# Halving the matmuls of an inverse row product by exchanging partitions with DMA

## The chip, the cores and the metric

One core of one Trainium2 chip. The metric is device time in microseconds (us) of one execution. A run gets a state: "slow" when it is over 1.5% above the fastest run of the same kernel, else "fast"; causes are read from fast runs. In the lines of the profile `ps` is a PSUM buffer, in which TensorE leaves its results, and `arena` the kernel's SBUF buffer, spread over 128 partitions; an *eviction* copies from `ps` to `arena`. SPq and ACTq are the issuing of transfers by SyncE and ScalarE. Where I name a ratio, it is the mean time of one kernel's fast runs over the mean of the other's fast runs of the same rounds, so it is not quite the ratio of the medians that stand beside it.

## The reference, cut to what matters

```python
xn = layernorm(A_x)                                   # 2048 x 640
X  = rfft2(xn)                                        # 2048 x 321, complex
y  = irfft2(X * (w_r + 1j * w_i), s=(2048, 640))      # the spectral filter
h  = (xn @ w_gate) * (xn @ w_up)                      # 640 -> 1536
out = A_x + y + h @ w_down                            # 2048 x 640
```

The kernel writes the transforms as matmuls with constant tables. The rows are split 2048 = 64 x 32. In the *spectrum stage* 16 steps each handle two groups of frequencies ("g" 0 and 1): a column product (forward), a forward row product, the filter product with the weights, and an inverse row product. Gate/up products are mixed in to fill TensorE.

## The kernel before: what the change touches

For every group the kernel multiplied the row product's PSUM result with both weights, real and imaginary, and formed the inverse as two accumulating passes over them. GpSimd, with some help of ScalarE and VectorE, made the negated copies that this needs.

```python
def em_wm(...):                       # VectorE, from PSUM, for one group q
    for h in range(2):                # 4 of 5 column classes, both weights at once
        c.e.tensor_tensor(dst, xh.unsqueeze(1).to_broadcast([128, 2, 32, 4]), wv, _OP.mult)
    return c.e.tensor_tensor(d5, x5, wg[:, :, 0:321:5], _OP.mult)      # the fifth class
def em_ng(...):                       # GpSimd, ScalarE or VectorE: negated copy
def em_ns(...):                       # GpSimd: two copies and a negation of 63 to 65 columns
def em_ia(...):                       # TensorE: ten matmuls for one group
    for k in range(5):
        l1, l2 = (yg[:, 578 + k:1090:4], yg[:, 322 + k:834:4]) if k < 4 else (yg[:, 0:128], yg[:, 128:256])
        c.e.matmul(dst, l1, v_ti[:, q, 0, :], start=True, stop=False)
        ins = c.e.matmul(dst, l2, v_ti[:, q, 1, :], start=False, stop=True)
# (cut: weights loaded straight from w_r and w_i, two to four transfers for each and every two steps)
# The order on each engine comes from a list planner in the kernel, which counts
_DMA_ISSUE = 500.0    # ns for SyncE to issue a transfer
_DMA_LAT = 1150.0     # ns from the last byte to the waiting engine
```

## Time and profile before

| | before |
|---|---|
| time, median of 3 (range) | 204.56 us (204.50 to 204.68) |
| TensorE busy | 198.0 us, 98% |
| VectorE / ScalarE / GpSimd busy | 89% / 63% / 16% |
| spectrum stage, 82.6 to 138.5 us | 55.9 us, TensorE busy 55.2 |

The lines and their reading are in the prediction.

### The profile page before, as it was taken

The numbers are of one execution on the slowest core, as the hardware profiler recorded it, in microseconds if no ns is written. First come the engines' busy times: TensorE is split into PE (matmuls) and PEld (weight loads), VectorE is DVE, ScalarE is ACT, GpSimd is POOL, SyncE is SP. The second block draws the span as 40 slices with busy tenths as digits, with TensorE's granted clock in tenths as the row PEclk, the third lists the DMA queues.
The fourth block names the chain that finished last, engine by engine and source line by source line (L and its number), as shares of the span: only waits on it lengthen the run. The fifth ranks groups of instructions, "written<-read, shape, count | busy, mean of one in ns | idle before, by whom it ended". The sixth has DMA issues, their size and how long they took to land.

```text
span 202.8 us, 4769 instructions
## 1 busy us (share of the span) xinstructions
PE 198.0 (98%) x1785; PEld 128.1 (63%) x1785; DVE 179.5 (89%) x511; ACT 127.5 (63%) x277; POOL 32.0 (16%) x108
## 2 busy tenths in 40 slices
PE   7999999999999999899999999999999999999995
PEld 7987644454444555556666666667777767777774
DVE  3599999999999997697988898864999999999983
ACT  3678899999975776869999999987611220200000
POOL 0000000000000000075754675453000000000000
DMA  6999983031161597605354444004313332332222
GB/s 183 300 341 378 377 80 65 3 65 32 32 63 39 112 276 194 197 14 132 74 145 114 103 102 127 0 5 136 92 32 97 106 107 66 113 90 81 93 65 65
DMA packets 31542, 23.82 MB, mean 117 GB/s; under 512 B 10528, under 2 KB 29472, under 8 KB 31392
## 3 DMA queue, kind: packets, MB, share of 16 engines
q1 hardware_dynamic: 30720, 23.16, 43.5%
q10 hardware_dynamic: 800, 0.36, 0.6%
q8 instruction: 14, 0.23, 0.5%
q14 instruction: 8, 0.07, 0.1%
HBM read 18.92 MB, written 2.62 MB: 106 GB/s over the span
## 4 chain that ended last, share of the span: by engine, by line
PE 85%; DVE 5%; SPq 4%; DMA 4%; issue 1%; ACT 1%
PE ps L978 44%; PE ps L1237 23%; SPq L712 4%; DMA arena<-in_A_x_dram 4%; PE ps L1131 3%; PE ps L1130 3%; PE ps L998 2%; PE ps L1079 2%; PE ps L938 2%; PE ps L1159 2%; PE ps L1249 2%; PE ps L1056 2%; DVE arena L719 1%; DVE arena L1257 1%; DVE arena L1186 0%
## 5 line engine op out<-in xcount | busy, mean ns | idle before, releaser
L718 ACT ACTIVATE arena<-ps 128x512 bf16<-128x512 f32 (+7 forms) x206 | 104.8, 547 | 40.1 <-PE ps L1159 24.0
L978 PE MATMUL ps<-arena 128*128 128x512 bf16 x420 | 97.0, 379 | 0.1
L978 PEld LDWEIGHTS ps<-arena 128*128 128x128 bf16 x420 | 38.9, 98 | 41.9 <-ACT arena L718 1.4
L1237 PE MATMUL ps<-arena 128*128 128x320 bf16 (+2 forms) x396 | 56.5, 295 | 0.2 <-DVE arena L1257 0.2
L1237 PEld LDWEIGHTS ps<-arena 128*128 128x128 bf16 x396 | 37.6, 98 | 13.9 <-DVE arena L1257 0.5
L1094 DVE TENSOR_TENSOR arena<-ps,arena 128x256 bf16<-128x256 f32 x64 | 24.0, 416 | 0.1
L1014 DVE TENSOR_TENSOR arena<-arena 128x512 bf16<-128x512 bf16 x42 | 17.7, 421 | 4.7 <-ACT arena L718 4.7
L1107 POOL TENSOR_SCALAR arena<-arena 128x256 bf16<-128x256 bf16 x8 | 6.8, 855 | 89.3 <-DVE arena L1097 89.2
L719 DVE CAST arena<-ps 64x321 bf16<-64x321 f32 (+1 forms) x25 | 12.2, 490 | 6.3 <-PE ps L1131 5.8
L1257 DVE TENSOR_TENSOR arena<-ps,arena 128x320 bf16<-128x320 f32 (+2 forms) x33 | 15.4, 473 | 1.8 <-PE ps L1249 1.8
L998 PE MATMUL ps<-arena 128*128 128x128 bf16 (+1 forms) x160 | 14.4, 246 | 0.4 <-ACT arena L718 0.4
L1130 PEld LDWEIGHTS ps<-arena 128*128 128x128 bf16 x160 | 12.4, 114 | 2.8 <-ACT arena L718 0.4
L998 PEld LDWEIGHTS ps<-arena 128*128 128x128 bf16 x160 | 12.0, 98 | 2.1 <-ACT arena L718 1.2
L1130 PE MATMUL ps<-arena 128*128 128x64 bf16 x160 | 13.3, 196 | 0.0
L1131 PE MATMUL ps<-arena 128*128 128x64 bf16 x160 | 13.3, 197 | 0.0
L1131 PEld LDWEIGHTS ps<-arena 128*128 128x128 bf16 x160 | 11.2, 113 | 2.1
L1116 POOL TENSOR_SCALAR arena<-arena 128x65 bf16<-128x65 bf16 x32 | 12.1, 378 | 0.0
L1114 POOL COPY arena<-arena 128x63 bf16<-128x63 bf16 x32 | 8.6, 268 | 17.1 <-DVE arena L1097 17.0
L1097 DVE TENSOR_TENSOR arena<-ps,arena 128x130 bf16<-128x130 f32 x32 | 9.3, 292 | 0.0
L776 ACT ACTIVATE arena<-arena 128x640 bf16<-128x640 bf16 x11 | 9.1, 824 | 0.0
L1115 POOL COPY arena<-arena 128x63 bf16<-128x63 bf16 x32 | 9.0, 280 | 0.0
L891 DVE TENSOR_TENSOR arena<-arena 128x384 f32<-128x384 bf16 x16 | 8.8, 552 | 0.0
(62 smaller groups left out, 221.0 us busy)
## 6 DMA issues: line engine op xcount, KB each, us to landing
arena<-in_A_x_dram SPq DMA_DIRECT2D x20, 160.0 KB, 2.4
out_dram<-arena SPq DMA_DIRECT2D x31, 80.0 KB, 1.6
arena<-in_A_w_r_dram SPq DMA_DIRECT2D x8, 160.5 KB, 3.0
arena<-in_A_w_i_dram SPq DMA_DIRECT2D x8, 160.5 KB, 3.0
arena<-in_B_w_gate_dram SPq DMA_DIRECT2D x4, 320.0 KB, 5.8
arena<-in_A_x_dram SPq DMA_DIRECT2D x1, 1280.0 KB, 9.8
arena<-in_A_w_r_dram SPq DMA_DIRECT2D x14, 80.2 KB, 2.9
arena<-in_A_w_i_dram SPq DMA_DIRECT2D x14, 80.2 KB, 3.1
```

Source lines behind the costliest of these rows:

```text
L718: return c.e.activation(dst, src, _ACTF.Copy)
L719: return c.e.tensor_copy(dst, src)
L978: ins = c.e.matmul(ps[:, bk, :], v_gw[:, w, j, ft, :], v_xt[:, j, rows], start=(j == 0), stop=(j == 4))
L998: ins = c.e.matmul(ps[:, bk, w * n:(w + 1) * n], v_gw[:, w, j, ft, :], v_xt[:, j, rows], start=(j == 0), stop=(j == 4))
L1014: return c.e.tensor_tensor(v_ht[:, ft0, rows], v_gbf[:, rr, 0, :], v_gbf[:, rr, 1, :], _OP.mult)
L1094: c.e.tensor_tensor(dst, xh.unsqueeze(1).to_broadcast([128, 2, 32, 4]), wv, _OP.mult)
L1097: return c.e.tensor_tensor(d5, x5, wg[:, :, 0:321:5], _OP.mult)
L1116: return c.e.tensor_scalar(yg[:, 128:193], yg[:, 256:321], -1.0, None, _OP.mult)
L1130: c.e.matmul(dst, l1, v_ti[:, q, 0, :], start=True, stop=False)
L1131: ins = c.e.matmul(dst, l2, v_ti[:, q, 1, :], start=False, stop=True)
L1237: ins = c.e.matmul(ps[:, bk, 0:sl3.stop - sl3.start], v_ht[:, ft, a * 128:(a + 1) * 128], v_wd[:, ft, sl3], start=(ft == _FT_ORDER[0]), st ...
L1257: return c.e.tensor_tensor(v_out[:, a % 2, sl3], ps[:, bk, 0:sl3.stop - sl3.start], v_xr[:, xs, sl3], _OP.add)
```

## The change

The intent: do the inverse in one pass, 160 matmuls in place of 320. One pass needs both parts of the product, which lie in different partitions, so the parts are brought together by DMA: the imaginary product is sent to its neighbour partition and added, and the mirrored half is fetched from the other 64 partitions. For this the weights have to lie in filter order with a sign for each partition; a one-time rearrangement through DRAM (26 copies) gives the order, and GpSimd multiplies the sign in. The last additions also move from VectorE to ScalarE copies with a bf16 addition. The diff, cut to its core:

```diff
-for g in range(2): em_wm, em_ng (negate), em_ns (copies), em_ia with ten matmuls
+d_w2 = nc.dram_tensor("w_slots", [2, _R // 2, 64, 2, 321], _BF).ap()
+for i_, (dst_, src_) in enumerate(prep):                      # 26 copies DRAM to DRAM, forward stage
+    dma("wprep%d" % i_, dst_, src_, ...)
+def em_ws(c, wi=v_wr[wr][:, :, 1, :]):                        # GpSimd, 8 times, 128 x 1284
+    return c.e.tensor_scalar(wi, wi, v_tau, None, _OP.mult)
+                                                              # VectorE: 4 products of 320, 2 of 4 (em_wa, em_wb)
+for i_ in range(2):                                           # first exchange: neighbours
+    dma("sw%d_%d" % (t, i_), qs[i_:128:2, :, 0:322], yb[1 - i_:128:2, :, 322:644], ...)
+def em_sum(c, yb=yb, qs=qs):                                  # VectorE
+    return c.e.tensor_tensor(yb[:, :, 0:322], yb[:, :, 0:322], qs[:, :, 0:322], _OP.add)
+for i_, (pd, psr, gs, k_) in enumerate(mv):                   # second exchange: halves (2 issues, 7 in step 0)
+    dma("ng%d_%d" % (t, i_), yb[pd, gs, 321:640], yb[psr, gs, 1:320], ...)
+def em_ia(...):                                               # TensorE: ten matmuls for BOTH groups
+            ins = c.e.matmul(ps[...], yb[:, g, o_:o_ + 636:5], v_ti[:, 2 * t + g, :], start=True, stop=True)
(cut: tables, buffers, order of the down weights, final additions)
```

## The prediction

> **What bounds the kernel now.** I read the page's busy shares first, then the chain that ended last, then the table of busy time by stage, then the timeline inside the stage that is rewritten.
>
> ```profile
> PE 198.0 (98%) x1785; PEld 128.1 (63%) x1785; DVE 179.5 (89%) x511; ACT 127.5 (63%) x277; POOL 32.0 (16%) x108
> ...
> PE 85%; DVE 5%; SPq 4%; DMA 4%; issue 1%; ACT 1%
> PE ps L978 44%; PE ps L1237 23%; SPq L712 4%; DMA arena<-in_A_x_dram 4%; PE ps L1131 3%; PE ps L1130 3%; PE ps L998 2%; PE ps L1079 2%; PE ps L938 2%; PE ps L1159 2%; PE ps L1249 2%; PE ps L1056 2%; DVE arena L719 1%; DVE arena L1257 1%; DVE arena L1186 0%
> ```
>
> TensorE is busy for 98% and carries 85% of the chain; no other engine has more than 5%. L978 is the gate/up product, L1237 the down product, and L1130/L1131 the two passes of the inverse row product, which the change halves.
>
> The stage table (us; PE, PEld, DVE, ACT, POOL busy, then clock, DMA share, GB/s):
>
> ```profile
> 18.00:82.60 64.60, 64.32 (x381) 32.89 (x382) 61.55 (x185) 54.43 (x116) 0.00 (x0) 1.00 0.54 128
> 82.60:138.50 55.90, 55.22 (x670) 34.16 (x667) 47.40 (x146) 51.33 (x119) 31.71 (x104) 1.00 0.35 88
> 138.50:163.40 24.90, 24.82 (x227) 18.66 (x224) 22.53 (x54) 8.28 (x14) 0.12 (x1) 1.00 0.30 87
> 163.40:202.80 39.40, 36.90 (x295) 27.02 (x293) 35.61 (x86) 2.60 (x4) 0.00 (x0) 1.00 0.28 84
> ```
>
> I call them forward, spectrum, combine and end. TensorE idles 0.3, 0.7, 0.1 and 2.5 us in them (the 2.5 is the last addition and store). So a change gains only by taking TensorE work away, and it loses whatever idle time it opens. The spectrum stage has VectorE (47.4) and ScalarE (51.3) close behind.
>
> The price of one inverse-row matmul is its spacing, not its duration:
>
> ```profile
> 104.98 0.19 PE L1130 MATMUL ps<-arena 128*128 128x64 bf16 x1
> 105.01 0.20 PE L1131 MATMUL ps<-arena 128*128 128x64 bf16 x1
> 105.04 0.20 PE L1130 MATMUL ps<-arena 128*128 128x64 bf16 x1
> ...
> 105.27 0.19 PE L1131 MATMUL ps<-arena 128*128 128x64 bf16 x1
> ```
>
> The ten start 32 ns apart. The groups view says 196 ns each, because these matmuls overlap.
>
> **What the Trainium skill says.** "TensorE: Matmul & The Clock Gate", "Wait — 56ns, not 53.3ns?", puts the warm spacing at N/2.4 ns plus 2.5 ns. For N=64 that is 29 ns; the trace has 32 ns here and 31 ns for the five of L1056. So the count of matmuls sets the price.
>
> "VectorE: DVE Perf Modes", "The perf-mode tier table", has any product with a float32 PSUM operand at one element a cycle and a bf16 tensor-tensor in SBUF at two. The trace agrees:
>
> ```profile
> L1094 DVE TENSOR_TENSOR arena<-ps,arena 128x256 bf16<-128x256 f32 x64 | 24.0, 416 | 0.1
> L1014 DVE TENSOR_TENSOR arena<-arena 128x512 bf16<-128x512 bf16 x42 | 17.7, 421 | 4.7 <-ACT arena L718 4.7
> L1097 DVE TENSOR_TENSOR arena<-ps,arena 128x130 bf16<-128x130 f32 x32 | 9.3, 292 | 0.0
> ```
>
> "SBUF — State Buffer", "SBUF: two separate sides", says GpSimd and a VectorE instruction with two SBUF inputs take a shared port pair in turn, for a whole instruction. The trace shows one direction: a GpSimd copy beside the VectorE product of L1014 is stretched from 0.23 to 0.44 us, while L1014 keeps its 0.42.
>
> ```profile
> 106.30 0.43 DVE L1014 TENSOR_TENSOR arena<-arena 128x512 bf16<-128x512 bf16 x1
> 106.38 0.44 POOL L1115 COPY arena<-arena 128x63 bf16<-128x63 bf16 x1
> ```
>
> The other direction, VectorE held by a long GpSimd instruction, is not in this trace, because GpSimd's are short.
>
> "DMA: Bandwidth & Descriptors", "Why a DMA increments its semaphore by 16 and not by 1", says a copy runs on the largest number of engines up to 16 that divides both outer dimensions. That explains the blocks of 15 or 16 outer rows. No run yet shows it.
>
> **The change, part by part.**
>
> *Inverse row product.* 320 matmuls become 160: 160 x 32 ns = 5.1 us off TensorE, all in the spectrum stage and on the chain (L1130 and L1131 hold 3% + 3% there, about 10.5 us for all 320). The forward matmuls widen from 321 to 326 columns: 32 x 5/2.4 ns = 0.07 us more. Everything else on TensorE keeps its count. Stage floor 55.9 - 5.1 = 50.8 us, or 3.2 us for each of the 16 steps.
>
> *VectorE in the spectrum stage.* From the timeline, spacing is the duration less about 80 ns: 0.34 us for L1094, 0.20 for L1097, 0.34 for L1014. Before: 64 x 0.34 + 32 x 0.20 for products, 18 x 0.34 for the gate products, 8 x 0.18 negations, 18 x 0.41 and 7 x 0.42 evictions: 46 us. After, one step has four products of 320 from PSUM (320/0.96 ns + 70 = 0.40 us), two of four elements (about 0.1) and one bf16 sum of 644 (644/2/0.96 ns + 70 = 0.40): 2.2 us, 16 times, 35.4. With 18 gate products (6.1) and the 14 evictions that the new order leaves it (5.7): 47 us. So VectorE goes from 46 of 55.9 to 47 of 50.8, 93%.
>
> *ScalarE.* It loses 16 negations (6.7 us). It takes all inverse evictions, 16 of 640 at about 0.70 us (11.2) in place of 25 of 320 at 0.436 (10.9), and 50 forward evictions in place of 46 (+1.7): 51.3 becomes about 47 of 50.8.
>
> *GpSimd.* 104 short instructions go. Eight sign products over 128x1284 come: 256 elements took 855 ns and 65 took 378, so 2.5 ns an element and 216 ns fixed: 3.4 us each, 27 us.
>
> *Exchanges.* A step now crosses partitions twice by DMA: product, exchange, sum, exchange, inverse. An 80 KB store here lands 1.6 us after issue and a 160 KB load in 2.4:
>
> ```profile
> arena<-in_A_x_dram SPq DMA_DIRECT2D x20, 160.0 KB, 2.4
> out_dram<-arena SPq DMA_DIRECT2D x31, 80.0 KB, 1.6
> ```
>
> Each exchange is two issues of 80 KB, so about 2.4 us from first issue to last landing. Chain of one step: 0.3 forward + 1.4 three products + 2.4 + 1 queueing + 0.4 sum + 2.4 + 0.5 = 8.4 us. The new order puts an inverse just ahead of the fourth forward product after its own, 3 to 4 steps or 9.5 to 12.7 us later. It fits, with 1 to 4 us spare.
>
> *Rearrangement.* 5.3 MB go through DRAM once more, during the forward stage, where DMA carries 20 to 70 GB/s. Bytes are no problem; order is. The first two copies are issued ahead of the last transpose that the second group of rows needs:
>
> ```profile
> 31.08 2.52 SPq L837 DMA_TRANSPOSE arena<-arena  x2
> ```
>
> That transpose leaves at 32.4 and lands by about 35.5; its matmuls begin near 37.2 (60 matmuls of 0.216 us and three short groups from 23.1). Two copies cost about 2 us to issue and 2 to 4 to move. The transpose then lands at 37 to 40: 0 to 3 us of idle TensorE, middle 1.
>
> *End.* Final additions: 30 products from PSUM (0.48 us) leave VectorE for 30 ScalarE copies and 15 bf16 additions (about 0.49): VectorE gains 7 us. TensorE is already busy there except for the tail, so 0 us. The down product may start before the inverse is done, behind which the last step's exchanges hide: four gate/up groups (4.3 us) and 20 down matmuls (2.7) stand between.
>
> *Sum.* 204.56 - 5.1 + 0.1 = 199.5 with no new idle time. I add 1 us for the transpose and 1 us for exchanges caught behind a weight load: each load is 330 KB into 64 partitions, two every other step, queued ahead of exchanges that have 1 to 4 us spare. Prediction 201.6.
>
> **The rivals.**
>
> *Everything hides: 199.5.* For it: 1 to 4 us spare in the chain, ScalarE relieved, seven eighths of the order unchanged. Against: it needs no idle time in a stage with VectorE at 93%.
>
> *The exchange latency becomes the bound.* Transfers run in one order on one issuing queue; one that waits for VectorE holds those behind it. If the chain takes 14 us and four spectrum buffers are in use, a step takes 3.5 us in place of 3.2: 16 x 0.3 = 5 us, time 204 to 206. For it: four buffers and two issues for every hop. Against: the hops measure 1.6 to 2.4 us.
>
> *GpSimd holds VectorE.* If a 3.4 us sign product blocks the next two-input VectorE instruction until it ends, each of about five in the stage costs some 2.3 us, 11 us on an engine with 3.5 spare: 8 us more, 208 to 210. For it: the skill's lock. Against: in the trace GpSimd is the one that waits, and VectorE keeps its 0.42 us.
>
> **Range and chances.** The floor of 199.5 can hardly be beaten, since TensorE's other work is the same; 198.6 allows for its present 1.1 us of idle before the tail. The top, 207, holds the latency rival and half of the GpSimd one. To be faster by over 2% (below 200.5) needs less than 1 us of new idle time: 0.33. Slower by over 2% (above 208.7) needs the GpSimd lock or a serial chain: 0.11. Between: 0.56.
>
> **What would show it.** Right: 160 inverse matmuls 32 ns apart; TensorE's sum about 193 us; spectrum stage 51 to 53 us from the first forward product to the last inverse; PSUM products of 320 near 0.48 us and the bf16 sum near 0.49; exchanges landing in under 2.5 us; sign products near 3.4 us, with L1014's successor still near 0.42. Wrong: TensorE waiting in the spectrum stage on a partition exchange for several us (latency), gate products or sums stretched to 1 us or more beside a sign product (lock), or matmuls near 37 us waiting on the transpose for more than 3 us. A time below 198.6 would mean that TensorE had hidden idle time that I counted as work.

## The result, and the profile after

The changed kernel is correct and took 230.89 us (median of 4, 227.33 to 233.07) against 204.53 (204.25 to 204.68) in the same rounds: ratio 1.117, 95% interval 1.110 to 1.123. I had predicted 201.6 and a range up to 207. Two of the four runs are slow; the two fast ones (227.33 and 229.76, middle 228.55) are 24 us slower than before.

The profiled execution of the changed kernel fell in the slow state (231.3 us span); profiles of its variants that did not (no_prep, sign_tiny and sign_vector below) show the same picture in the parts that they keep, so I read it for where the time lies and take sizes from the fast runs. Its page has, in the same places as before, the busy shares and the chain by engine:

```profile
PE 205.2 (89%) x1625; PEld 126.3 (55%) x1625; DVE 184.0 (80%) x492; ACT 139.5 (60%) x287; POOL 28.7 (12%) x12
...
DVE 32%; PE 30%; DMA 18%; SPq 12%; ACT 3%; issue 3%; POOL 2%; DVEq 0%; POOLq 0%
```

The number of matmuls fell by 160 as meant. But TensorE went from 85% of the chain to 30%; DMA and SyncE's issuing (SPq) together have 30%, and VectorE 32%. No engine is full on average. This is the mark of a chain of waits that goes from engine to engine.

The table by stage of the changed kernel (start:end, length, then busy us of PE, PEld, DVE, ACT, POOL, clock, DMA share, GB/s; forward, spectrum, combine, end):

```profile
18.00:84.00 66.00, 63.63 (x361) 31.97 (x362) 61.66 (x184) 52.46 (x113) 0.00 (x0) 0.97 0.86 169
84.00:168.20 84.20, 64.74 (x567) 35.10 (x564) 57.24 (x144) 54.33 (x105) 28.47 (x8) 0.95 0.63 152
168.20:190.00 21.80, 21.39 (x170) 15.43 (x169) 18.32 (x42) 10.07 (x19) 0.00 (x0) 0.87 0.21 58
190.00:231.30 41.30, 38.93 (x311) 28.58 (x309) 34.25 (x81) 11.70 (x26) 0.00 (x0) 1.00 0.27 83
```

The spectrum stage took 84 us in place of 56; in the forward stage TensorE stood for 2.4 us in place of 0.3, and the rest is nearly as before. So the question is the spectrum stage. The chain in order of time shows what fills it (start, us, what; a piece of a step in the middle of the stage):

```profile
115.48 0.61 SPq L725
116.09 0.04 issue
116.13 4.29 DMA arena<-arena
...
126.73 3.88 DMA arena<-arena
130.61 0.02 issue
130.63 0.50 DVE arena L1161
131.13 0.34 DVE arena L1033
...
131.59 3.29 DMA arena<-arena
```

`arena<-arena` are the exchanges. The two exchanges of a step stand one after the other with the addition (L1161) between them, 3.3 to 4.3 us each, and no TensorE work appears between. And the timeline shows the addition held at a GpSimd sign product:

```profile
97.07 3.53 POOL L1088 TENSOR_SCALAR arena<-arena 128x1284 bf16<-128x1284 bf16 x1 [2.31 <-DMA arena<-w_slots]
...
97.96 2.53 DVE L1161 TENSOR_TENSOR arena<-arena 128x644 bf16<-128x644 bf16 x1
```

GpSimd ends at 97.07 + 3.53 = 100.60 us, and the addition, which takes 0.49 us elsewhere, at 100.49. So there were three suspects: the sign products, the exchanges, and the rearrangement, which seemed to make the first weights late.

### The profile page after: what moved, and what is told of

It is laid out like the page before. It is cut to its first block, busy times and chain, and to the rows that moved or that the text cites. A ratio compares the mean times of both kernels' runs of the same rounds, so it can differ in the third digit from the quotient of the medians.

```text
span 231.3 us, 4369 instructions
## 1 busy us (share of the span) xinstructions
PE 205.2 (89%) x1625; PEld 126.3 (55%) x1625; DVE 184.0 (80%) x492; ACT 139.5 (60%) x287; POOL 28.7 (12%) x12
## 4 chain that ended last, share of the span: by engine, by line
DVE 32%; PE 30%; DMA 18%; SPq 12%; ACT 3%; issue 3%; POOL 2%; DVEq 0%; POOLq 0%
PE ps L1291 22%; SPq L725 11%; DMA arena<-arena 11%; DVE arena L1033 5%; DVE arena L1139 4%; DVE arena L1161 4%; DMA arena<-in_A_x_dram 3%; DVE arena L1146 3%; PE ps L992 3%; DMA arena<-w_slots 3%; DVE arena L904 2%; PE ps L1213 2%; ACT arena L731 2%; PE ps L1303 2%; POOL arena L1088 2%
## 5 line engine op out<-in xcount | busy, mean ns | idle before, releaser
L731 ACT ACTIVATE arena<-ps 128x512 bf16<-128x512 f32 (+7 forms) x232 | 121.7, 555 | 81.7 <-PE ps L992 28.3
L992 PEld LDWEIGHTS ps<-arena 128*128 128x128 bf16 x420 | 39.9, 100 | 51.9 <-issue 8.0
L1291 PEld LDWEIGHTS ps<-arena 128*128 128x128 bf16 x396 | 38.2, 100 | 15.1 <-ACT arena L731 0.6
L1088 POOL TENSOR_SCALAR arena<-arena 128x1284 bf16<-128x1284 bf16 x8 | 28.5, 3562 | 115.0 <-DMA arena<-w_slots 115.0
L1161 DVE TENSOR_TENSOR arena<-arena 128x644 bf16<-128x644 bf16 x16 | 12.8, 807 | 9.6 <-DMA arena<-arena 9.6
L1139 DVE TENSOR_TENSOR arena<-ps,arena 128x320 bf16<-128x320 f32 x32 | 14.2, 484 | 5.3 <-PE ps L1129 5.2
L1183 PE MATMUL ps<-arena 128*128 128x64 bf16 x160 | 9.0, 205 | 10.4 <-DMA arena<-arena 10.2
L1183 PEld LDWEIGHTS ps<-arena 128*128 128x128 bf16 x160 | 7.9, 130 | 15.7 <-DMA arena<-arena 11.7
L1146 DVE TENSOR_TENSOR arena<-ps,arena 128x320 bf16<-128x320 f32 x32 | 15.2, 480 | 0.0
L1017 PE MATMUL ps<-arena 128*128 128x128 bf16 (+1 forms) x160 | 14.4, 246 | 0.5 <-ACT arena L731 0.5
L1017 PEld LDWEIGHTS ps<-arena 128*128 128x128 bf16 x160 | 12.0, 98 | 2.2 <-ACT arena L731 1.3
L1330 DVE TENSOR_TENSOR arena<-arena 128x640 bf16<-128x640 bf16 x15 | 7.3, 486 | 4.8 <-ACT arena L731 4.8
L1129 PE MATMUL ps<-arena 128*128 128x326 bf16 x32 | 7.2, 313 | 3.5 <-POOL arena L1088 2.8
L1100 PEld LDWEIGHTS ps<-arena 128*128 128x128 bf16 x160 | 7.6, 103 | 4.2 <-DVE arena L1149 0.9
L789 ACT ACTIVATE arena<-arena 128x640 bf16<-128x640 bf16 x11 | 9.0, 822 | 0.0
L1100 PE MATMUL ps<-arena 128*128 128x64 bf16 (+1 forms) x160 | 8.4, 201 | 0.4 <-DVE arena L1149 0.4
L780 ACT ACTIVATE arena<-arena 128x640 bf16<-128x640 bf16 x11 | 8.1, 735 | 1.0 <-DMA arena<-in_A_x_dram 0.9
```

The lines of the kernel that those rows point to most:

```text
L731: return c.e.activation(dst, src, _ACTF.Copy)
L992: ins = c.e.matmul(ps[:, bk, :], v_gw[:, w, j, ft, :], v_xt[:, j, rows], start=(j == 0), stop=(j == 4))
L1017: ins = c.e.matmul(ps[:, bk, w * n:(w + 1) * n], v_gw[:, w, j, ft, :], v_xt[:, j, rows], start=(j == 0), stop=(j == 4))
L1088: return c.e.tensor_scalar(wi, wi, v_tau, None, _OP.mult)
L1100: ins = c.e.matmul(dst, v_uq[:, k, t, :], v_fd[:, k * 128 + w * n: k * 128 + w * n + n], start=True, stop=True)
L1139: return c.e.tensor_tensor(yb[:, :, 322 * w + 161:322 * w + 321].rearrange("p g (m k) -> p g m k", k=5), xh, wv[:, :, :, 9:4:-1], _OP.mult)
```

## The experiments

Every experiment but sign_vector, deep_rings and two_queues gives a wrong result. Where an edit removes a wait or joins two transfers, the planner makes another order of instructions. By the traces there are three orders among these wrong-result runs: that of the changed kernel itself (sign_tiny, no_prep, sign_prep, short_exch); one for every run without exchanges (no_exchange, sign_exch, exch_prep, all_off, lock_own, floor, stride_one); and one for a single transfer a hop (one_issue, half_alone, half_short). So the sign products and the rearrangement are judged at one order, but the exchanges are never taken out without a change of order. The names s, e, p stand for taking away the large sign product, the exchanges and the rearrangement (the preparation).

### Each part taken away alone

```diff
s  -def em_ws(c, wi=v_wr[wr][:, :, 1, :]):
s  +def em_ws(c, wi=v_wr[wr][:, 0:1, 1, 0:8]):          # 8 columns in place of 1284
e  -dma("sw...", qs[...], yb[...]);  dma("ng...", yb[...], yb[...])
e  +# no exchange; SUM adds yb's own second half
p  -dma("wprep...", ...)  x26 ; loads from w_slots
p  +# loads of the same size from w_r and w_i as they lie, not before the last transpose
one_issue  -two transfers of 64 rows for each hop
one_issue  +one transfer of 128 rows for each hop, straight across
```

> The changed kernel, with each of the eight GpSimd sign products cut to 8 columns (wrong result on purpose); same order of instructions on every engine, same waits. Three theories. GpSimd lock: VectorE's sums and gate products lost 8.9 us beside GpSimd (16 sums at 807 ns in place of 487, 42 gate products at 510 in place of 420) and the first forward product waits 3.5 us for its weights' sign, so if the lock leads, the time falls by 12 us or more, to 218 or less. Exchange: if the two partition exchanges of each step set its length, the lost VectorE time is waiting time anyway and only the 3.5 us at the start come back, 226 to 228. Late weights: like the exchange theory here, 226 to 228. In each case the sums should be back at 0.49 us and the gate products at 0.42.

> The changed kernel without the partition exchanges: the sum adds the second half of its own row and the inverse reads the row as it is (wrong result on purpose). Exchange theory: 62 issues of 0.62 us and about 22 us in which TensorE waited on an exchange go; the spectrum stage falls from 84 us towards 60 and the time to 206 to 212. GpSimd lock theory: VectorE is held as before, and the time stays above 218. Late weights theory: at least the 6 us at the start of the stage stay, so the time is not below 206.

> The changed kernel without the rearrangement in DRAM: the weight loads read rows of the input of the same size and shape, but the wrong ones (wrong result on purpose). Late weights theory: the first forward product came at 91.4 us in place of 85.1 before, because 26 copies and the last transpose stood ahead of the weight loads, and the forward stage lost 2.1 us at 37 us to a transpose behind two copies: 6 to 9 us go, 220 to 224. Exchange and lock theories: the later steps are bound otherwise and catch up with part of that, 224 to 229; the 2.1 us at 37 us go in any case.

> The changed kernel with every exchange done by one transfer of 128 partitions that permutes nothing (wrong result on purpose): same bytes, same two crossings in a row, half the issues. If what the exchanges cost is the issuing queue (62 issues of 0.62 us are 38 us, with the weight loads about 49 us of a stage whose TensorE work is 51), half of the exchange cost goes: 216 to 222. If it is the landing time of 2.3 us and more, only the second issue of a pair is saved on each crossing, 0.6 us of about 4: 224 to 229.

Measured: sign_tiny 228.73 (228.07 to 229.67), no_exchange 224.00 (222.43 to 225.53), no_prep 230.89 (229.22 to 233.78), one_issue 232.95 (231.69 to 234.86). Against the fast runs of the changed kernel (228.55) only no_exchange gives something back, 4.6 us of 24; sign_tiny gives nothing (0.2 us slower), the fast runs of no_prep (230.85) are 2.3 us slower and one_issue 4.4. (The 2 to 7 of 26 in the text recorded next come from the medians of all runs, two of them slow.) no_prep and one_issue lie above every range that I had given for them. Taken one by one, no cause seems worth much. Several causes that mask one another would look like this.

### Each part left alone

> Both sign products cut and exchanges out, rearrangement kept (wrong result on purpose). After the first four runs each part alone gave back only 2 to 7 us of 26, so my new theory is that they stand in series only in part and hide each other: with one gone, the next one sets the step. Masking theory: the two together give back far more than 2 + 7, about 16 us, to 210 to 214, of which 6 to 8 is the late start of the weights. Rival (something else, such as the order of instructions, the pairs of PSUM banks or the TensorE clock, sets the time): not below 218.

> Sign products cut and rearrangement out, exchanges kept (wrong result on purpose). Masking theory with exchanges that land 3.4 to 5 us after issue: two crossings of some 4.5 us, two VectorE parts of about 2 us and four buffers, which gives a step of 3.8 to 4.3 us and 215 to 222. If late weights and the lock together were the whole loss: 205 to 208. Rival (order or clock): not below 222.

> Exchanges and rearrangement out, sign products kept on GpSimd (wrong result on purpose). Masking theory: eight sign products of 3.5 us hold VectorE up to 3.5 us each at the next instruction with two SBUF inputs; where they fall in the spectrum stage that is 10 to 12 us on an engine with 3 us spare, 208 to 214. If the lock cost nothing here: 200 to 203. Rival (order or clock): not below 218.

> All three out: only the one-pass inverse, the new layout, the paired PSUM banks and the new final additions are left (wrong result on purpose). If the floor of the prediction holds (204.5 less 5.1 for 160 matmuls), 199 to 202. If the order, the paired banks or the clock carry a part of the loss, 204 or more, and the prediction's floor was wrong too.

| run | what is left of the three | us, median (range) | fast runs: median (number) | ratio to before | fast runs above all_off |
|---|---|---|---|---|---|
| after | all | 230.89 (227.33 to 233.07) | 228.55 (2) | 1.117 | 24.2 |
| sign_tiny | exchanges, rearrangement | 228.73 (228.07 to 229.67) | 228.73 (4) | 1.117 | 24.4 |
| no_exchange | sign products, rearrangement | 224.00 (222.43 to 225.53) | 224.00 (4) | 1.094 | 19.7 |
| no_prep | sign products, exchanges | 230.89 (229.22 to 233.78) | 230.85 (3) | 1.125 | 26.6 |
| sign_exch | rearrangement | 209.83 (208.85 to 212.72) | 209.54 (3) | 1.024 | 5.2 |
| sign_prep | exchanges | 221.58 (217.23 to 222.32) | 217.23 (1) | not given: one fast run | 12.9 |
| exch_prep | sign products | 222.68 (222.19 to 223.73) | 222.68 (4) | 1.089 | 18.4 |
| all_off | nothing | 204.30 (204.27 to 205.13) | 204.30 (4) | 0.999 | 0 |

Here is the whole loss. Sign products alone cost 18 us and the rearrangement alone 5, each at the order of all_off. Exchanges alone cost 13 us by the one fast run of sign_prep (its other three, at 221.4 to 222.3, count as slow), and a change of order is in this figure. They add to 36, and together they cost 24, so some waits lie beside one another. The table shows which. Exchanges and rearrangement together (sign_tiny) already cost 24.4, no less than apart: these two do not mask each other. The sign products add 18.4 us where neither of the two stands, and nothing where both do. So the masking is between the sign products and the other two.

exch_prep missed my range (208 to 214) and fell into that of its rival, "order or clock: not below 218". The order is ruled out: all_off has the same instructions in the same order on TensorE, VectorE and ScalarE and takes 204.3. The clock is taken up below. All three away, the time is that of the kernel before, no better, although 160 matmuls are gone. That is a second finding, followed up below.

The rearrangement's cost is to be seen in the chain of sign_exch, which has neither sign product nor exchange:

```profile
87.04 1.08 PE ps L992 x5
88.17 12.59 DMA arena<-w_slots
101.30 0.72 PE ps L1129 x4
```

Every load from the rearranged weights waits for all 26 copies. The first two were issued from 83.15 us on and had landed at 88.56; the first forward row product (L1129) started at 89.18, where all_off has 85.28. The load in the chain is the sixth: it took 12.6 us to land (100.76), and the row products behind it started at 101.30, where all_off has 96.89. In the changed kernel the first row product started at 91.39 us, 6.3 us later than the 85.1 of before, but this is not the rearrangement's doing alone: no_prep, which has none, starts it at 91.55, and exch_prep, with sign products alone, at 91.70.

### What the sign product does: lock or latency

Two explanations for the 18 us of exch_prep: the row products wait 3.5 us for their weights to be signed, or GpSimd blocks VectorE. In lock_own the sign product writes to a buffer that nothing reads, so nothing waits for it.

```diff
-return c.e.tensor_scalar(wi, wi, v_tau, None, _OP.mult)      # in place, products wait
+return c.e.tensor_scalar(wo, wi, v_tau, None, _OP.mult)      # to an own buffer, nobody waits
```

> exch_prep with its eight GpSimd sign products writing to a buffer that nothing reads, so that no row product waits for them (wrong result on purpose). Same count, size and place of GpSimd instructions. Port lock: GpSimd holds VectorE's two-input instructions whether or not anyone wants its result, so the time stays far above the 204.3 us of all_off: 214 to 223, with sums, gate products or other two-input VectorE instructions of 1.5 to 3.5 us beside a GpSimd product. Rival, latency: the 18 us that exch_prep had over all_off are row products that wait 3.5 us for the sign product behind each weight load; then this run is at 204 to 206. Both: 208 to 213.

Measured: 217.81 us (216.62 to 221.45; the three fast runs 217.36), ratio 1.064 (1.061 to 1.067), profiled in a fast run. So of the 18.4 us, 13 are there although nobody wants the result; and since the profiled run took 216.62 us at a clock of 1.000, as all_off has, and the order is the same, neither clock nor order explains 12 of them. The other 5 may be the wait for the signed weights, but that is not shown: exch_prep also ran at a lower TensorE clock (0.969 to 0.977; lock_own's fast runs 0.976 to 1.000), and no run separates the two. The timeline of lock_own:

```profile
97.85 1.00 DVE L733 CAST arena<-ps 64x326 bf16<-64x326 f32 x2
98.47 3.53 POOL L1090 TENSOR_SCALAR arena<-arena 128x1284 bf16<-128x1284 bf16 x1 [7.02 <-DMA arena<-in_A_w_i_dram]
98.88 2.94 DVE L1034 TENSOR_TENSOR arena<-arena 128x512 bf16<-128x512 bf16 x1
101.86 0.49 DVE L1141 TENSOR_TENSOR arena<-ps,arena 128x320 bf16<-128x320 f32 x1
```

The gate product L1034, which takes 0.42 us, started 0.41 us after GpSimd and ended at 101.82; GpSimd ended at 102.00. What reads PSUM (L1141, L1148, the CAST) keeps its usual time beside GpSimd:

```profile
113.32 3.53 POOL L1090 TENSOR_SCALAR arena<-arena 128x1284 bf16<-128x1284 bf16 x1 [6.92 <-DMA arena<-in_A_w_i_dram]
...
114.24 0.48 DVE L1141 TENSOR_TENSOR arena<-ps,arena 128x320 bf16<-128x320 f32 x1
114.64 2.10 DVE L1160 TENSOR_TENSOR arena<-arena 128x644 bf16<-128x644 bf16 x1
```

Here L1141 runs in 0.48 us inside the GpSimd instruction, and the addition after it is held until 116.74, GpSimd's end being 116.85. This is the lock that the Trainium skill describes in "SBUF — State Buffer", "SBUF: two separate sides": an exclusive lock, held for a whole instruction by whichever starts first. This run agrees, for VectorE instructions with two SBUF operands: ten of them start inside a sign product; eight end 0.18 us (gate products) or 0.11 us (additions) before it does, and the two that start in its last 0.3 us keep their time. By groups, gate product, addition and a product from PSUM (count | busy us, mean ns), first all_off, then lock_own:

```profile
L1033 DVE TENSOR_TENSOR arena<-arena 128x512 bf16<-128x512 bf16 x42 | 17.5, 418 | 5.0 <-ACT arena L731 4.8
...
L1147 DVE TENSOR_TENSOR arena<-ps,arena 128x320 bf16<-128x320 f32 x32 | 15.1, 478 | 0.0
...
L1159 DVE TENSOR_TENSOR arena<-arena 128x644 bf16<-128x644 bf16 x16 | 7.8, 489 | 0.3
```

```profile
L1034 DVE TENSOR_TENSOR arena<-arena 128x512 bf16<-128x512 bf16 x42 | 28.1, 668 | 4.9 <-ACT arena L732 4.8
...
L1148 DVE TENSOR_TENSOR arena<-ps,arena 128x320 bf16<-128x320 f32 x32 | 15.1, 478 | 0.0
...
L1160 DVE TENSOR_TENSOR arena<-arena 128x644 bf16<-128x644 bf16 x16 | 11.5, 716 | 0.3
```

VectorE's busy sum rises from 174.7 us in all_off to 188.8 in lock_own, 14.1 us, against 13 us of time: VectorE is busy for 55.3 of the 55.9 us from 82.6 to 138.5 us there, so the holds come through nearly whole.

### The repair that lies at hand

```diff
-T("WS_%d" % t, opts.get("ws_eng", ("pool",)), ...)
+T("WS_%d" % t, opts.get("ws_eng", ("dve",)), ...)
```

> The changed kernel, right result, with the eight sign products given to VectorE in place of GpSimd; the planner makes its own order anew (it plans 206.3 us in place of 205.7). The three causes mask one another, so taking the GpSimd ones away alone gives back as little as sign_tiny did: 226 to 231. If GpSimd were the one cause that matters and sign_tiny was a fluke: 210 to 216. VectorE pays 8 x about 0.5 us = 4 us, mostly in waits that exist anyway.

Measured: correct, 228.88 us (228.28 to 230.33), ratio 1.119. As sign_tiny says: with the lock gone from a correct kernel, exchanges and late weights hold the same time.

### What the exchanges cost: bytes, round trips or the issuing queue

short_exch leaves the exchanges alone (like sign_prep) and cuts each from 322 or 319 columns to 8. half_alone and half_short issue each hop as one transfer in place of two, with all columns and with 8.

```diff
short_exch  -qs[i_:128:2, :, 0:322], yb[1 - i_:128:2, :, 322:644]
short_exch  +qs[i_:128:2, :, 0:8],   yb[1 - i_:128:2, :, 322:330]
half_alone  -for i_ in range(2): dma("sw...", 64 rows);  for ... in mv: dma("ng...", 64 rows)
half_alone  +dma("sw...", qs[:, :, 0:322], yb[:, :, 322:644]);  dma("ng...", yb[:, :, 321:640], yb[:, :, 1:320])
```

> sign_prep (exchanges alone left, 221.6 us in a slow profile) with every exchange cut from 322 or 319 columns to 8, the same number of transfers, the same waits and the same order (wrong result on purpose). Theory, round trips: the cost is the fixed time of a transfer and the order of issue, two in series for each of 16 steps, so 1/40 of the bytes changes little: 215 to 222, with landings of 2 us or more. Rival, bytes and contention of the 16 engines: landings fall below 2 us and the time goes to 204 to 209.

> sign_prep (exchanges alone left, 217 to 222 us) with each hop issued as one transfer of 128 rows in place of two of 64, straight across without the swap of partitions: the same bytes, two issues for a step in place of four (wrong result on purpose; the planner makes its own order, 202.8 us). Issuing queue as the bound: 11 issues in two steps become 7, 4.5 us in place of 7.2, and the time falls to 204 to 212. Round trip of each transfer as the bound: 215 to 221.

> half_alone with 8 columns in place of 322 or 319 (wrong result on purpose). Compared with short_exch (216.0 us), which has twice the issues. Queue as the bound: 203 to 208. Round trip as the bound: 212 to 216.

| exchanges alone | 322 columns | 8 columns |
|---|---|---|
| two issues a hop | 217.23 (sign_prep, its one fast run) | 216.04 (215.31 to 216.66) |
| one issue a hop | 210.50 (210.10 to 210.85) | 207.57 (206.91 to 209.52) |

Against the 204.3 of all_off. The largest part is not bytes: halving the issues gives 8.5 us with short transfers, where all runs are fast, and 6.7 with full ones by the one fast run of sign_prep; cutting the bytes by 40 gives 1.2 or 2.9. What neither takes away is 3.3 us. (Three reservations: the median of all four runs of sign_prep is 221.58; half_alone has no swap of partitions and its planner made another order; and with half the issues each hop also lands one issue, 0.65 us, sooner, so the work of the queue and the length of a step's chain are not told apart.) My expectation of short_exch, that the round trip was the cost, held for the number; half_short, at 207.57 inside the range that I had given for the queue (203 to 208), speaks against the reason. SyncE's queue in sign_prep, merged (start, us, what, how many):

```profile
102.56 5.17 SPq L725 DMA_DIRECT2D arena<-arena  x8
107.77 0.64 SPq L725 DMA_DIRECT2D arena<-in_A_w_r_dram  x1
108.45 0.63 SPq L725 DMA_DIRECT2D arena<-in_A_w_i_dram  x1
```

Eight exchange issues, two steps' worth, in 5.17 us without a gap, and two weight loads behind: 0.65 us an issue. This is the fullest stretch. From the first exchange issue to the end of the last (86.74 to 152.57 us) the queue's records are 84 issues, 69 of exchanges, 10 of weights and 5 others, never two at once; they take 53.3 of the 65.8 us, 81% (in short_exch, a fast profile, 53.0 of 61.6), where I had put the floor of the whole stage at 50.8. In half_alone the same stretch has 47 issues, 28.9 of 53.9 us, 54%. So issuing nearly fills the queue in one run and not in the other; the rest of the queue's time is waiting.

one_issue had shown nothing of this. That the lock and the late weights masked it there is argued, not shown.

### Two attempts on a correct kernel

deep_rings: sign products on VectorE, five spectrum buffers for four, three receive buffers for two, and a planner that knows 0.62 us an issue and 2.6 us a landing.

```diff
-_DMA_LAT = 1150.0 ; _DMA_ISSUE = 500.0 ; _NY = 4 ; _NS = 2
+_DMA_LAT = 2600.0 ; _DMA_ISSUE = 620.0 ; _NY = 5 ; _NS = 3
```

> The changed kernel, right result, with the sign products on VectorE, five spectrum buffers in place of four, three receive buffers in place of two, and the planner told 0.62 us for an issue and 2.6 us for a landing in place of 0.5 and 1.15; it plans 216.5 us. If exchange and order could be hidden with more buffers: 205 to 212. If the two hops in series on one issuing queue, with the late weights, are what limits: 216 to 226, less than the 228.9 of sign_vector by what the truer order saves. If the order was never the matter: 227 to 230.

Measured: correct, 228.16 us (226.86 to 229.74), ratio 1.115: no gain over sign_vector's 228.88, and in the range that I had given for "the order was never the matter" (227 to 230), not in that of my theory (216 to 226). Buffers and a truer plan gained nothing here.

two_queues: sign products on VectorE, and the second exchange issued from ScalarE's queue.

```diff
-dma("ng%d_%d" % (t, i_), ..., reads=yk(0, 3))
+dma("ng%d_%d" % (t, i_), ..., reads=yk(0, 3), q="act")
```

> The changed kernel, right result, with the sign products on VectorE and the second exchange of each step issued from ScalarE's queue in place of SyncE's; the planner plans 216.2 us, as it counts an issue as ScalarE time. If the one issuing queue is what limits: 214 to 225, below the 228.9 of sign_vector by several us. If not, or if the issues cost ScalarE as much as they save: 226 to 233.

Measured: correct, 239.23 us (238.76 to 240.63), ratio 1.170: worse by 10 us than sign_vector, and above both ranges that I had given. ScalarE's timeline shows why (ACTq is its issuing):

```profile
100.43 10.16 ACTq L725 DMA_DIRECT2D arena<-arena  x11
110.64 0.60 ACT L731 ACTIVATE arena<-ps 128x512 bf16<-128x512 f32 x1 [9.87 <-DVE arena L1161]
```

An issue that must wait for the addition holds every eviction behind it on that engine: ScalarE stood for 9.87 us here. A second queue on an engine that has work is no free queue.

### Where the gain of 160 matmuls went

all_off has the new one-pass inverse and no new cost, and takes the time of the kernel before. Its chain from 83 us on is a row of ScalarE evictions:

```profile
85.77 0.92 ACT arena L731 x2
86.70 0.44 ACT arena L731
87.14 0.02 issue
87.16 0.43 ACT arena L731
```

and the step of the stationary operand (the one that TensorE loads before a matmul; here every fifth element) shows in the spacing. floor takes both away, stride_one the step alone:

```diff
stride_one, floor  -yb[:, g, o_:o_ + 636:5]
stride_one, floor  +yb[:, g, 128 * k:128 * k + 128]
floor              -copy_on(c, v_a[..., 328 * g:328 * g + _LP], ps[..., 0:_LP])
floor              +copy_on(c, v_a[..., 328 * g:328 * g + 8], ps[..., 0:8])
```

> all_off (204.3 us) with two more things taken away: the forward evictions copy 8 columns in place of 326 (same instructions, same order), and the inverse product's stationary operand is read without its step of 5 elements (wrong result on purpose). Theory: all_off had TensorE work removed but waited for the forward evictions at the start of the spectrum stage; now 199 to 202, and the ten inverse matmuls start 32 ns apart in place of 39. Rival: the order of the plan itself leaves TensorE idle for as long as it works less: 203.5 to 205. If the step is not what set 39 ns, the spacing stays at 39.

> all_off (204.3 us) with the inverse product's stationary operand read in one piece in place of every fifth element, and nothing else (wrong result on purpose); evictions are whole again. If the step of 5 is what makes the ten matmuls start 39 ns apart, they start 32 ns apart here, which is 16 x 10 x 7 ns = 1.1 us: 203 to 203.6. If the evictions were the bound, nearly all of the 3.7 us that floor won stays lost: 203 to 204.3. If the step was the bound: 200.5 to 202.

Measured: floor 200.65 us (200.41 to 201.19), ratio 0.981 (0.979 to 0.982); stride_one 203.93 (203.72 to 204.42), ratio 0.996 (0.993 to 0.999). The ten inverse matmuls of a step as one merged piece, first all_off, then stride_one:

```profile
110.69 0.55 PE L1181 MATMUL ps<-arena 128*128 128x64 bf16 x10
```

```profile
112.17 0.46 PE L1181 MATMUL ps<-arena 128*128 128x64 bf16 x10
```

Less the last one's duration (203 and 194 ns in the groups view), nine spacings: 39 ns with the step, 30 ns without. That is 16 x 10 x 9 ns = 1.4 us of TensorE work, of which 0.4 us came out as time. The remaining 3.3 us came with the forward evictions, 52 of 64 of them on ScalarE. So even with no exchange at all, the evictions, and by the chain those of ScalarE, held TensorE at the start of the stage. No version that I ran with a right result beats the kernel before.

## Why the prediction was wrong

The prediction named all three of the mechanisms that cost time, and gave each a size that was too small: 2 us in the sum, against 24 measured. By its own steps:

1. *"1 us for exchanges caught behind a weight load"*. The exchanges were worth 13 us by themselves (one fast run, a change of order in it). The chain of 8.4 us was summed from landings, and beside it the step "Each exchange is two issues of 80 KB, so about 2.4 us from first issue to last landing" treated issuing as latency only. The landings were not the error: their median in the changed kernel is 2.3 us, though those on its chain above took 3.3 to 4.3. I never summed the issues as work of an engine. The trace of before had their price, three weight loads of the spectrum stage on SyncE's queue, 0.61 us each:

```profile
118.15 1.84 SPq L712 DMA_DIRECT2D arena<-in_A_w_r_dram  x3
```

   Times the 84 issues, this is 51 us against a floor of 50.8; in sign_prep they took 53.3. That this work of the queue is the cost, and not the chain that it lengthens, is likely but not told apart. The rival "exchange latency becomes the bound" pointed the right way ("two issues for every hop"), with 204 to 206 us as its price in place of 217.

2. *"GpSimd is the one that waits, and VectorE keeps its 0.42 us."* This was the reason to give the lock half a weight in the range, and it was a reading of one direction only, with GpSimd instructions of 0.2 to 0.9 us. What starts first holds the other; a 3.5 us instruction gives VectorE far longer to run into it. The rival had counted about five sign products in the stage and 11 us of holds, of which 3.5 would be spare, 8 in all. In the changed kernel all eight lie in the stage (87.7 to 143.9 us). The rival's mechanism is shown by lock_own; the size there is 14.1 us of holds and 13 of time. exch_prep has 5 us more, in which the wait for the signed weights, which I had not put in the sum at all, and the clock are not separated.

3. *"Bytes are no problem; order is."* I applied this to one transposed block near 37 us (middle 1 us; TensorE stood for 2.1 us there, inside my 0 to 3). The costlier order was at the other end: the weight loads wait for all 26 copies, and in sign_exch the first forward row product came 3.9 us later than in all_off, those behind the sixth load 4.4. By itself the rearrangement cost 5.2 us. Nor is it shown that bytes were no problem: the DMA share of the forward stage went from 0.54 to 0.86, and the sixth load took 12.6 us to land in sign_exch, where loads of its size have medians of 4.3 and 5.1 us in sign_prep.

4. *"Stage floor 55.9 - 5.1 = 50.8 us."* With every new cost away the time was 204.3, not 199.5. The 32 ns were taken from a stationary read with a step of 4; with a step of 5 the spacing was 39, so the gain was 320 x 32 - 160 x 39 ns = 4.0 us. And *"ScalarE ... about 47 of 50.8"* was a sum over the stage; in all_off the chain runs through ScalarE's evictions without a break from 83.5 to 95.4 us, the first 12 us. Only with evictions cut did the time come to 200.65.

5. TensorE's clock was not in the prediction. In sign_vector, a fast profile, the granted clock was 0.94 in the spectrum stage (84 to 168 us), where TensorE stood for 18.5 us, and 0.97 in the mean. The Trainium skill ("TensorE: Matmul & The Clock Gate", "What's actually happening") has the clock follow how busy TensorE was. The traces here don't settle it: all_off and half_alone, with less idle time, stayed at 1.00, but so did the profiled run of lock_own, in which TensorE stood for 14.4 of the 55.9 us from 82.6 to 138.5 us. Within one kernel a lower clock came with a longer time (sign_prep: 217.23 us at 0.992, 221.40 to 222.32 at 0.969 to 0.977). How many of the 24 us are clock, no run here separates.

What held: products from PSUM of 320 at 0.48 us, the bf16 addition at 0.49 where it was free, sign products at 3.53 us for a predicted 3.4, 160 matmuls fewer, little gained or lost at the end. The unit costs were near, but for the spacing in point 4; the sums over shared resources, the issuing queue, the port pair and ScalarE at the stage's start, were missing or averaged.

## What to carry to other kernels

Count DMA issues as work of the engine that issues them: number of issues times their duration in the trace, against the length of the stage, before any talk of latency. Put no long GpSimd instruction that reads SBUF beside a VectorE that is nearly full: a hold came through nearly whole here (13 of 14 us), and the trace of short GpSimd instructions did not show it. When taking away one suspect gives nothing, take away all and put back one at a time; each of three causes here looked like less than 5 us one way and like 5 to 18 the other. Compare the orders of instructions too, where a planner makes a new one.

## What the Trainium skill lacked or had wrong

- "DMA: Bandwidth & Descriptors", "Issuing engines are not separate DMA queues", says that the time to initiate a DMA "is usually small relative to the DMA itself". Here it was 0.61 to 0.65 us an issue on SyncE's queue beside a median landing of 2.5 us, but 84 of them took 53.3 of 65.8 us, and halving the issues was worth 7 to 8.5 us where the exchanges stood alone (217.2 to 210.5, 216.0 to 207.6), with a new order in the figure. The page's advice has a second side that it lacks: issuing from ScalarE cost 10 us (228.9 to 239.2), since a waiting issue holds that engine's evictions, 9.87 us in one place.
- "SBUF — State Buffer", "SBUF: two separate sides", was right about the lock, also in that it names only VectorE instructions with two SBUF inputs (or in a mode that uses both ports): those with one operand in PSUM ran at their usual 0.48 us beside the same GpSimd instruction. What it lacks is what a hold looks like: 2.94 us in place of 0.42, busy time and not idle time in the profile.
- "SBUF — State Buffer", "Door 1: The DMA port swizzle", in its note on 16-byte lines, says that bf16 can be strided over 8 elements for free. For TensorE's stationary operand a step of 5 was not free: 39 ns between matmuls in all_off, 30 in one piece in stride_one, and its weight loads took 131 and 98 ns (medians). Nor does a limit of 4, which the note's own parenthesis (two hits for each line) would give, quite fit: in the kernel before, where eight of ten were read with a step of 4, the spacing was 32 and the loads took 115 ns.
- "TensorE: Matmul & The Clock Gate", "Wait — 56ns, not 53.3ns?": the warm spacing for 64 columns works out as 29 ns, and stride_one's 30 ns agrees; the page does not say what a step in the stationary operand adds, 9 ns a matmul here.
